# Attention beside a long convolution: the products of the last 128 convolution channels made later, and other paces for the convolution

## The chip, the cores and the metric

The kernel runs on one core of one Trainium2 chip. The metric is device time in microseconds (us); the median of seven runs of the kernel before is 862.89 us (860.53 to 865.09). One further execution was profiled. The engines are called PE (TensorE), ACT (ScalarE), DVE (VectorE), POOL (GpSimd) and SP (SyncE, which here only issues transfers).

## The reference

Two independent results stand side by side in the output, 512 columns each. The first is attention over 2048 positions with 32 heads of 16:

```python
qkv = (x @ wqkv).reshape(B, S, 3, H, Dh)           # S = 2048, H = 32, Dh = 16
p = softmax(einsum("bhqd,bhkd->bhqk", q, k) * Dh ** -0.5)
a = einsum("bhqk,bhkd->bhqd", p, v)  @ wo           # heads joined first
```

The second is a gated long convolution over 512 channels. The keys pass a causal filter of four taps, are multiplied by the values, and the product `kv` is convolved causally, channel by channel, with a filter as long as the sequence (in the reference by FFT):

```python
k_shift = sum(k_pad[:, t:t + S, :] * shift_k[:, 3 - t] for t in range(4))
kv = k_shift * v
y = causal_conv(kv, ssm_k) + kv * ssm_D             # 512 filters of 2048 taps
b = q * y
out = concatenate([a, b], axis=-1)
```

## The kernel before

**Attention.** Scores are cut into 2048 blocks of 128 keys by 512 queries (4 query blocks, 8 groups of 4 heads, 16 key tiles, 4 heads). A step T takes three blocks, or two: before step `N_EARLY` = 184 every odd step has two, later three steps in every 21 (the slots, which begin at step 190) and the last few. There are 741 steps. In a step `emit_qk` (line 539) makes the scores on PE, ACT makes the exponentials of the step in one instruction (line 550), and two steps later PE multiplies by the values (line 632). From step 56 on one of three blocks may go to DVE instead, which makes the exponential in five instructions (lines 586, 593 three times, 598); `dve_block` decides by how much work the planner has already given to DVE. When the sums of a group of heads are complete, DVE transposes them (line 696), divides by the row sum and, after two groups, transposes back into OTN (line 718). PE then multiplies by the output weights (line 749).

**Convolution.** The filters are reversed on DVE (`kz_turn`, line 426), with `ssm_D` added to one tap, and written to a scratch in DRAM (`kz_store`). From there SP loads, for each channel, 128 shifted copies of the filter, a row of WR of 512 KB. Four channels make a quad; three quads fit into WR, and `load_wr` issues the four loads of the next quad when a place comes free. `conv_lags` (line 804) makes the convolution of a quad as 16 lags, each of four small matmuls, one for each channel in its own quarter of PE. After eight quads `conv_turn` (line 830) transposes the result, and DVE multiplies it by q.

**The products kv.** The 512 channels are four blocks c of 128. A unit `("kv", c, i)` makes a quarter of a block: 16 matmuls (line 355) of the transposed keys in KTR with diagonal tap matrices DG, issued in two halves of eight, and one multiplication by the values on DVE (line 393). The buffers are shared with other things. KTR[0], for blocks 0 and 1, lies in QN; KTR[1], for blocks 2 and 3, lies in the second half of the query buffer QT. The values lie in WR, VS2 and OUTA. DG lies in rows 4 to 7 of OTN, one row for each block. Therefore the first write of the second half of QT (`evac_unit`, kind "q", qb = 1) and the transpose back for p = 4 (`turn_back`) wait for the last kv product (`h_kvm`). A quad of channels can only be convolved when all four kv units of its block are done.

**The order.** The program is written out in order by a planner in the kernel itself. Each engine has a planned clock; `us=(...)` in a call is what the planner counts for an instruction. `dma` counts a transfer as `kb/DMA_KB` us after the one before, or 3.6 us plus that after its issue. Units (v, k, q, kv, op, turn) are put in where there is room. `unit_step` takes the head of the list `early` before step 184 and issues half of it when `fits` says that it ends before the scores of the next step must start, with `SPARE` = 0.1 us to spare; a unit that is due is issued without room ("forced"). After step 184 units may only go into the slots, and `next_unit` takes the one with the earliest due time; in the steps 1 and 3 of a slot it is forced from 42 steps before its due time. `emit_bg` gives the convolution what is left: at most `LAGS` lags a step, as many as `room` allows (the end of the running exponential, less 0.47 us and `MARGIN`), and as many as the pace has credited. The credit grows by `PACE` times the lags left over the time left (1.14 us a step until 16 steps before the end), at most `RATE` = 3.4 lags/us. A quad is taken up only if its loads have landed by the planner's count. `KZ_LATE` is the time that the filter reversals wait after the filter has landed, by the same count.

All transfers of WR, and the transposing loads of keys and x, are issued by SP in program order; POOL issues the loads of q and of the output weights and most of the output. At the end `op_out_end` copies four tiles of the output, two on ACT (line 767) and two on DVE (line 769), and issues one transfer for each.

## Time and profile before

| | |
|---|---|
| median of 7 runs | 862.89 us (860.53 to 865.09) |
| the profiled execution | 869.32 us; its span 867.6 us, mean PE clock 0.977 |
| ACT busy | 837.7 us, 97% |
| DVE busy | 783.3 us, 90% |
| PE busy | 745.3 us, 86% |
| exponentials on ACT (line 550) | 741, of which 354 of three blocks (1569 ns) and 386 of two (1158 ns) |
| blocks on DVE (line 598) | 213 |
| matmuls of the convolution (line 804) | 8192 |
| loads of WR from the scratch | 512 of 512 KB, 8.0 us to landing (median) |
| DMA | 289.36 MB, mean 334 GB/s |
| kv units: DVE products (line 393) | 16, from 80.4 to 184.6 us; block 3 from 169.9 to 184.6 |
| PE waits for WR before line 804 | 10.7 us in 18 pieces, and 21.0 us before its weight loads |

Step 184 lies at about 205 us: the load of the output weights, which is issued there, starts at 205.2. "Busy" is the time in which an engine executes; PE's ends are modelled, and its weight loads are counted apart, since they run beside the matmuls. A time "from A to B" counts from the start of the span. The granted clock is the share of full speed that PE was given.

### The profile page before, as it was taken

Reading aid. Unit: us, or ns where it says so; the run is one execution under the profiler, and the core shown is the slowest. Engines: PE = TensorE matmul, PEld = TensorE weight load, DVE = VectorE, ACT = ScalarE, POOL = GpSimd, SP = SyncE. Lnnn points to the kernel's source line nnn. Section 1 sums busy time; section 2 is a strip of 40 time slices with the busy share of each in tenths; the row PEclk is TensorE's granted clock in tenths of the full one; section 3 lists DMA queues with packets and bytes.
Section 4 is the critical chain, followed back from the end, with each engine's and each line's share of the span. In section 5 each row is a group of like instructions: output and inputs, shape, how many; then the busy total and the mean of one; then the engine's idle time right before and its main releaser. Section 6 shows DMA issues by size and latency. Waiting matters only on the chain.

```text
span 867.6 us, 29386 instructions
## 1 busy us (share of the span) xinstructions
PE 745.3 (86%) x13146; PEld 304.8 (35%) x13184; DVE 783.3 (90%) x1330; ACT 837.7 (97%) x746; POOL 17.3 (2%) x33
## 2 busy tenths in 40 slices
PE   8888899998888888888888898888888888888877
PEld 2223343443333333333333323333333333333332
DVE  2328999999999999998999979989999999999994
ACT  6999999999999999998999979989999999999997
POOL 2000000000000000000000010000000000000000
PEclk9999999999999999999999969989999999999999
DMA  9960069779999999999999989989999999999942
GB/s 271 261 227 1 8 209 340 271 242 344 407 408 407 385 402 389 409 396 409 351 395 376 345 333 391 385 309 385 408 408 393 383 402 407 407 392 408 407 197 73
DMA packets 104813, 289.36 MB, mean 334 GB/s; under 512 B 35184, under 2 KB 37232, under 8 KB 104304
## 3 DMA queue, kind: packets, MB, share of 16 engines
q1 hardware_dynamic: 99424, 279.35, 85.8%
q0 software_dynamic: 1808, 6.29, 2.1%
q8 instruction: 104, 1.70, 0.8%
q10 hardware_dynamic: 3456, 1.84, 0.8%
q14 instruction: 21, 0.17, 0.1%
HBM read 276.83 MB, written 6.42 MB: 326 GB/s over the span
## 4 chain that ended last, share of the span: by engine, by line
ACT 62%; DVE 15%; PE 10%; DMA 9%; issue 2%; SPq 1%; ACTq 0%
ACT PT L550 62%; DMA WR<-kz_scratch 8%; DVE EH L593 7%; PE PS L539 4%; DVE FX L586 3%; DVE PTD L598 3%; PE PS L632 2%; PE PS L804 2%; SPq L223 1%; DVE QT L380 1%; DMA xT<-in_A_x_dram 1%; PE PS L363 1%; PE PS L749 1%; DVE DT L696 1%; PE PS L830 0%
## 5 line engine op out<-in xcount | busy, mean ns | idle before, releaser
L550 ACT ACTIVATE PT<-PS 128x1536 bf16<-128x1536 f32 (+1 forms) x741 | 834.7, 1354 | 17.7 <-PE PS L539 17.3
L539 PE MATMUL PS<-QT,KTo 32*128 32x512 bf16 x2048 | 306.9, 390 | 88.4 <-ACT PT L550 71.9
L593 DVE SCALAR_TENSOR_TENSOR EH<-EH,FX 128x512 f32<-128x512 f32 x426 | 285.4, 688 | 0.0
L804 PE MATMUL PS<-WR,KV 128*5 128x128 bf16 (+15 forms) x8192 | 224.0, 222 | 13.8 <-DMA WR<-kz_scratch 10.7
L632 PE MATMUL PS<-PT,VAF 128*32 128x512 bf16 x1835 | 203.8, 396 | 3.8 <-DVE DT L696 2.9
L804 PEld LDWEIGHTS PS<-WR,KV 128*2 128x2 bf16 (+15 forms) x8192 | 150.2, 88 | 98.8 <-issue 44.1
L539 PEld LDWEIGHTS PS<-QT,KTo 32*128 32x128 bf16 x2048 | 73.1, 91 | 268.9 <-ACT PT L550 228.1
L586 DVE TENSOR_SCALAR FX<-PS 128x512 f32<-128x512 f32 x213 | 147.3, 692 | 10.6 <-PE PS L539 10.3
L598 DVE SCALAR_TENSOR_TENSOR PTD<-EH,FX 128x512 uint16<-128x512 f32 x213 | 145.6, 686 | 0.0
L593 DVE SCALAR_TENSOR_TENSOR EH<-FX 128x512 f32<-128x512 uint16 x213 | 145.2, 691 | 0.0
L632 PEld LDWEIGHTS PS<-PT,VAF 128*32 128x32 bf16 x1835 | 48.6, 93 | 120.9 <-issue 108.2
L1012 PE MATMUL PS<-IDN,ZW 128*32 128x512 bf16 (+3 forms) x229 | 72.7, 318 | 1.2 <-DVE QN L839 0.9
L632 PE MATMUL PS<-PTD,VAF 128*32 128x512 bf16 x213 | 61.4, 390 | 0.0
L405 DVE CAST VAF<-PS 128x512 bf16<-128x512 f32 x16 | 11.1, 692 | 30.2 <-PE PS L363 30.2
L696 DVE STREAM_TRANSPOSE DT<-PS 128x512 f32<-128x512 f32 x31 | 22.3, 718 | 13.3 <-PE PS L632 12.6
L1012 PEld LDWEIGHTS PS<-IDN,ZW 128*32 128x32 bf16 x229 | 22.1, 97 | 12.0 <-issue 10.7
L380 DVE TENSOR_SCALAR QT<-PS,MASK 128x512 bf16<-128x512 f32 x30 | 21.2, 750 | 3.0 <-PE PS L335 2.8
L819 DVE CAST YB<-PS 128x512 bf16<-128x512 f32 x32 | 22.0, 689 | 0.6 <-PE PS L804 0.4
L363 PE MATMUL PS<-WKV,xT 128*128 128x512 bf16 x59 | 17.7, 383 | 2.6 <-DVE VAF L405 1.5
L749 PE MATMUL PS<-WKV,OTN 128*128 128x512 bf16 x53 | 17.7, 397 | 2.1 <-issue 1.1
L344 PE MATMUL PS<-xT,WKV 128*128 128x512 bf16 (+1 forms) x57 | 16.7, 376 | 2.0 <-issue 1.0
L335 PE MATMUL PS<-xT,WQ 128*128 128x512 bf16 x46 | 15.2, 388 | 2.4 <-issue 1.9
(66 smaller groups left out, 199.7 us busy)
## 6 DMA issues: line engine op xcount, KB each, us to landing
WR<-kz_scratch SPq DMA_DIRECT2D x512, 512.0 KB, 8.0
kz_scratch<-WR SPq DMA_DIRECT2D x1, 2176.0 KB, 8.5
QN<-in_B_q_dram POOLq DMA_DIRECT2D x2, 1024.0 KB, 12.7
out_dram<-QN POOLq DMA_DIRECT2D x2, 1024.0 KB, 7.5
out_dram<-OUTA POOLq DMA_DIRECT2D x12, 128.0 KB, 5.4
QN<-in_B_ssm_k_dram SPq DMA_DIRECT2D x1, 1024.0 KB, 6.2
QT<-in_B_ssm_k_dram SPq DMA_DIRECT2D x1, 1024.0 KB, 8.2
WR<-in_B_v_dram SPq DMA_DIRECT2D x2, 512.0 KB, 7.4
```

The source lines that it names most:

```text
L363: return e.matmul(PS[:, bank, :], lhsT=xT[:, dc, kt * 128:(kt + 1) * 128], rhs=WV[:, dc, :], start=(dc == 0), stop=(dc == 3))
L380: lambda e, par=par: e.tensor_scalar(QT[:, qb % 2, 2 * o + par, :], PS[:, bank, :], MASK[:, par:par + 1], None, ALU.mult),
L539: ins = e.matmul(PS[:, bank, :], lhsT=KTo[32 * s:32 * s + 32, g // 2, kt * 128:(kt + 1) * 128], rhs=QT[32 * s:32 * s + 32, qb % 2, g, :], ...
L550: h_exp[T] = act.op(lambda e: e.activation(PT[:, T % R_PT, 0:n * QB], PS[:, banks[0]:banks[0] + n, :].rearrange("p b f -> p (b f)"), ACT.E ...
L586: h_f = urgent(lambda e: e.tensor_scalar(fx, PS[:, bank, :], FIX_ADD, FIX_HI, ALU.add, ALU.min), [h, h_last.get(i - R_FX)], slack=0.6)
L593: st["h"] = dve.op(lambda e: e.scalar_tensor_tensor(eh, src, (A3, A2, A1)[j], frac, ALU.add, ALU.mult), [st["h"], h_last.get(i - R_EH), h_ ...
L598: lambda e: e.scalar_tensor_tensor(out16, eh, A4, fx, ALU.mult, ALU.add),
L632: ins = e.matmul(dst, lhsT=w, rhs=rhs, start=(k == 0), stop=(k == KT - 1), tile_position=(0, 32 * s))
L696: h_t = urgent(lambda e: e.transpose(out=dt, in_=PS[:, pvb(n), :]), [h] + before, slack=0.1, us=(0.63, 0.751))
L749: ins = e.matmul(PS[:, bank, :], lhsT=OTN[:, (4 * qb + o) % R_O, t * 128:(t + 1) * 128], rhs=WO[:, o, :], start=(o == 0), stop=(o == 3))
L804: ins = e.matmul(PS[32 * c:32 * c + NB - n, BGB, 128 * (kk % 4):128 * (kk % 4) + 128], lhsT=KV[:, qd, n:NB, c], rhs=WR[:, r + c, 128 * (NB ...
L1012: pe.op(lambda e: e.matmul(PS[32 * s:32 * s + 32, pvb(n), 0:128 * k], lhsT=ZW[:, :], rhs=rhs, start=False, stop=False, tile_position=(0, 3 ...
```

## The change

The key weights WK and the value weights WV change places in the buffer WKV, which gets 16 more columns. The keys of the convolution now come in three loads: blocks 0 and 1 as before (1024 KB), block 2 alone in the query buffer, and block 3 alone in the place of the key weights, which are no longer needed once the last key product k(3,3) is made; that load waits for this product. The values of blocks 2 and 3 change places. The four kv units of block 3 leave the list `early` and become jobs for the slots with the due time `KV_DUE` = 300. `h_kvm` is split: the query buffer and the transpose p = 4 wait for block 2, the transpose p = 7 for block 3.

Numbers: at most 5 lags a step instead of 6; PACE 1.15 instead of 1.2; before step 184 the lags keep a margin of 0.2 us instead of 0.35 (`EARLY_MARGIN`); KZ_LATE 8 instead of 4. At the end the transfer of output tile 1 is issued by SP instead of ACT.

```diff
--- before.py
+++ after.py
@@ -35,8 +35,8 @@
 PVB = 6
 BGB = 7
 N_EARLY = 184
-LAGS = 6
-PACE = 1.2
+LAGS = 5
+PACE = 1.15
 KEYS0 = 256
 END = 16
 
@@ -63,10 +63,12 @@
 GAP = 7
 TAIL_GAP = 4
 AHEAD = 4
-KZ_LATE = 4.0
+KZ_LATE = 8.0
 KEEP = 4
 BACKLOG = 3.9
 MARGIN = 0.35
+EARLY_MARGIN = 0.2
+KV_DUE = 300
 SPARE = 0.1
 DMA_KB = 400.0
 WINDOW = 3.4
@@ -175,7 +177,7 @@
     WQ = sb("WQ", [128, 4, D])
     PAT = sb("PAT", [1, 2, 128])
     MASK = sb("MASK", [128, 2], FP32)
-    WKV = sb("WKV", [128, 2, 4, D])
+    WKV = sb("WKV", [128, 8 * D + LEFT])
     OTN = sb("OTN", [128, R_O, QB])
     DT = sb("DT", [128, QB], FP32)
     DTN = sb("DTN", [128, 2, QB])
@@ -190,15 +192,17 @@
     EH = sb("EH", [128, R_EH, QB], FP32)
     ZW = sb("ZW", [128, 32])
     JNK = sb("JNK", [128, 2], FP32)
-    WK = WKV[:, 0, :, :]
-    WV = WKV[:, 1, :, :]
+    WK = WKV[:, 4 * D:8 * D].rearrange("p (c f) -> p c f", c=4)
+    WV = WKV[:, 0:4 * D].rearrange("p (c f) -> p c f", c=4)
     WO = WV
     VST = [x.rearrange("p (t d) -> p t d", t=NB)
-           for x in (WR[:, 8, :], WR[:, 9, :], VS2[:, :], OUTA[:, :, :].rearrange("p r d -> p (r d)"))]
+           for x in (WR[:, 8, :], WR[:, 9, :], OUTA[:, :, :].rearrange("p r d -> p (r d)"), VS2[:, :])]
     KZS = WRF[:, 0:4 * LKZ].rearrange("p (c m) -> p c m", c=4)
     DSS = WRF[:, 4 * LKZ:4 * LKZ + 4].rearrange("p (c m) -> p c m", m=1)
     KTR = [QNF[:, 0:2 * LKR].rearrange("p (c s) -> p c s", c=2),
-           QTF[:, NG * QB:NG * QB + 2 * LKR].rearrange("p (c s) -> p c s", c=2)]
+           QTF[:, NG * QB:NG * QB + LKR].rearrange("p (c s) -> p c s", c=1),
+           WKV[:, 4 * D:4 * D + LKR].rearrange("p (c s) -> p c s", c=1)]
+    KT_OF = [(0, 0), (0, 1), (1, 0), (2, 0)]
     DG = OTN[:, 4:8, :].rearrange("p t d -> p (t d)").rearrange("p (c m d) -> p c m d", c=4, m=4)
     KZN = [QTF[:, NG * QB:NG * QB + 2 * S].rearrange("p (c s) -> p c s", c=2),
            QNF[:, 0:2 * S].rearrange("p (c s) -> p c s", c=2)]
@@ -256,7 +260,7 @@
 
     d_w = [DmaSem(sem(f"d_w{i}")) for i in range(5)]
     d_x = [DmaSem(sem(f"d_x{i}")) for i in range(4)]
-    d_kv = [DmaSem(sem(f"d_kv{i}")) for i in range(6)]
+    d_kv = [DmaSem(sem(f"d_kv{i}")) for i in range(7)]
     d_tap, d_kz, d_kzw, d_wo = [DmaSem(sem(n)) for n in ("d_tap", "d_kz", "d_kzw", "d_wo")]
     d_q = [DmaSem(sem(f"d_q{i}")) for i in range(2)]
     d_outB = [DmaSem(sem(f"d_outB{i}")) for i in range(2)]
@@ -288,10 +292,10 @@
     h_vn, h_kt, h_kt0 = [], {}, {}
     for c in range(4):
         src = bass.AP(tensor=v2.tensor, offset=v2[128 * (NB - 1), 128 * c].offset, ap=[[D, 128], [-128 * D, NB], [1, 128]])
-        h_vn.append(dma(sp, d_kv[2 + c], VST[c], src, kb=1024))
+        h_vn.append(dma(sp, d_kv[3 + c], VST[c], src, kb=1024))
 
     def load_kt(i, dep):
-        h_kt[i] = dma(sp, d_kv[i], KTR[i][:, :, LEFT:LEFT + S], k2[:, 256 * i:256 * i + 256], [dep], transpose=True, kb=1024)
+        h_kt[i] = dma(sp, d_kv[i], KTR[i][:, :, LEFT:LEFT + S], k2[:, (0, 256, 384)[i]:(256, 384, 512)[i]], [dep], transpose=True, kb=(1024, 512, 512)[i])
         h_kt0[i] = pool.op(lambda e: e.memset(KTR[i][:, :, 0:LEFT], 0.0), [dep])
 
 
@@ -320,7 +324,7 @@
         if u[0] == "k":
             return h_x[u[2]] + [h_wk[min(u[1], 1)]]
         if u[0] == "kv":
-            return [h_kt[u[1] // 2], h_dg[0]]
+            return [h_kt[KT_OF[u[1]][0]], h_dg[0]]
         return h_x[u[1] // 4] + [h_wv]
 
     def pe_unit(u, bank, dcs=(0, 1, 2, 3)):
@@ -345,14 +349,15 @@
                                 rhs=xT[:, dc, sc * 512 + c0:(sc + 1) * 512], start=(dc == 0), stop=(dc == 3))
         elif kind == "kv":
             _, c, i = u
-            deps += [h_kt[c // 2], h_kt0[c // 2], h_dg[0]]
+            kt_i, kt_c = KT_OF[c]
+            deps += [h_kt[kt_i], h_kt0[kt_i], h_dg[0]]
             mm_us, mm_run = 0.27, 0.21
 
             def mm(e, b):
                 ins = None
                 for m in range(4):
                     c0 = LEFT + 128 * (4 * i + 3 - b) - m
-                    ins = e.matmul(PS[:, bank, 128 * b:128 * b + 128], lhsT=KTR[c // 2][:, c % 2, c0:c0 + 128], rhs=DG[:, c, m, :],
+                    ins = e.matmul(PS[:, bank, 128 * b:128 * b + 128], lhsT=KTR[kt_i][:, kt_c, c0:c0 + 128], rhs=DG[:, c, m, :],
                                    start=(m == 0), stop=(m == 3))
                 return ins
         else:
@@ -385,6 +390,8 @@
             hh = urgent(lambda e: e.tensor_copy(KTo[:, o, sc * 512 + c0:(sc + 1) * 512], PS[:, bank, c0:512]), [h],
                         us=(0.335, 0.46) if c0 else V512)
             h_k[(o, sc)] = hh
+            if (o, sc) == (3, 3):
+                load_kt(2, h)
         elif kind == "kv":
             _, c, i = u
             dst = KV[:, 32 * c:32 * c + 32, NB - 4 - 4 * i:NB - 4 * i, :]
@@ -396,8 +403,10 @@
                 load_qn(0, [h])
                 wr_free.append((2, hh))
                 load_wr()
-            if sum(kv_n) == 16:
+            if c == 2 and kv_n[c] == 4:
                 h_kvm[0] = h
+            if c == 3 and kv_n[c] == 4:
+                h_kvm[1] = h
         else:
             _, kt = u
             dst = VAF[:, kt, 0:H * VW].rearrange("p (h e) -> p h e", e=VW)[:, :, 0:DH]
@@ -408,7 +417,7 @@
 
     h_kvc = [None] * 4
     kv_n = [0] * 4
-    h_kvm = [None]
+    h_kvm = [None, None]
     wr_free = []
     wr_next = [0]
     h_kzw = [None]
@@ -715,10 +724,12 @@
                 deps += [h_op[((p - R_O) // 4, t)] for t in range(4)]
             if p == 4:
                 deps.append(h_kvm[0])
+            if p == 7:
+                deps.append(h_kvm[1])
             h_otn[(p, i1)] = h_otn[p] = dve.op(lambda e: e.transpose(out=OTN[:, p % R_O, sl], in_=dtn[:, sl]), deps, us=us)
 
         def may_turn():
-            return 2 * p in h_mul and 2 * p + 1 in h_mul and (p < R_O or all(((p - R_O) // 4, t) in h_op for t in range(4)))
+            return 2 * p in h_mul and 2 * p + 1 in h_mul and (p != 7 or kv_n[3] == 4) and (p < R_O or all(((p - R_O) // 4, t) in h_op for t in range(4)))
         u_r, u_m, u_t = (0.155, 0.28), (0.334, 0.46), (0.6, 0.75)
         if last:
             recip(u_r)
@@ -768,7 +779,7 @@
         else:
             hh = dve.op(lambda e: e.tensor_copy(dst, PS[:, bank, :]), [h])
         r0 = qb * QB + t * 128
-        dma(act if t % 2 else sp, d_outE, out2[r0:r0 + 128, 0:D], dst, [hh])
+        dma(act if t == 3 else sp, d_outE, out2[r0:r0 + 128, 0:D], dst, [hh])
 
 
     h_wr, h_qn = {}, {}
@@ -853,14 +864,14 @@
     early += [(91, ("k", 2, 0)), (92, ("q", 0, 2)), (98, ("k", 2, 1)), (104, ("k", 2, 2)), (110, ("k", 2, 3))]
     early += [(130, ("kv", 1, i)) for i in range(4)]
     early += [(137, ("q", 0, 3)), (138, ("k", 3, 0)), (144, ("k", 3, 1)), (150, ("k", 3, 2)), (155, ("k", 3, 3))]
-    early += [(N_EARLY - 4, ("kv", c, i)) for c in (2, 3) for i in range(4)]
+    early += [(N_EARLY - 4, ("kv", c, i)) for c in (2,) for i in range(4)]
     later_q = [("q", qb, o) for qb in range(1, NQB) for o in range(4)]
     later_op = [(qb, t) for qb in range(NQB - 1) for t in range(4)]
-    state = {"qd": 0, "lag": 0, "turn": False, "q": 0, "op": 0, "started": False, "lags": 0.0,
+    state = {"qd": 0, "lag": 0, "turn": False, "q": 0, "op": 0, "kv": 0, "started": False, "lags": 0.0,
              "left": C // 4 * NB, "t": 0.0}
 
     def room(T):
-        end = at(h_exp[min(T, NT - 1)]) - 0.47 - MARGIN
+        end = at(h_exp[min(T, NT - 1)]) - 0.47 - (EARLY_MARGIN if T < N_EARLY else MARGIN)
         return end - max(pe.t, at(bank_free[BGB]))
 
     def group_step(qb, g):
@@ -884,6 +895,8 @@
             u = later_q[st["q"]]
             if u[1] < 2 or (u[1] - 2) * NG + 2 * u[2] + 1 in pv_done:
                 jobs.append((group_step(u[1], 2 * u[2]), u))
+        if st["kv"] < 4:
+            jobs.append((KV_DUE, ("kv", 3, st["kv"])))
         return min(jobs) if jobs else None
 
     def fits(T, start, us):
@@ -1036,7 +1049,7 @@
         emit_bg(T)
         warm_up(T)
         advance(pe.t)
-    assert state["qd"] == C // 4 and not state["turn"] and state["q"] == len(later_q) and state["op"] == len(later_op), state
+    assert state["qd"] == C // 4 and not state["turn"] and state["q"] == len(later_q) and state["op"] == len(later_op) and state["kv"] == 4, state
     assert not early_dve and not flow and not acts and not dves
```

## The prediction

> **What bounds the kernel now.** I read the page first (shares, chain, groups), then the busy time in stretches of 20 us, then the worst stretch in steps of 2 us, then the waits.
>
> ```profile
> PE 745.3 (86%) x13146; PEld 304.8 (35%) x13184; DVE 783.3 (90%) x1330; ACT 837.7 (97%) x746; POOL 17.3 (2%) x33
> ...
> ACT 62%; DVE 15%; PE 10%; DMA 9%; issue 2%; SPq 1%; ACTq 0%
> ...
> L550 ACT ACTIVATE PT<-PS 128x1536 bf16<-128x1536 f32 (+1 forms) x741 | 834.7, 1354 | 17.7 <-PE PS L539 17.3
> ```
>
> ACT, which computes the exponentials (line 550), works 97% of the span, and the chain that ended last lies 62% on it. Each of the 2048 score blocks costs either ACT or DVE: 213 blocks go to DVE (five instructions each), the rest to ACT. A three-block exponential takes 1569 ns and a two-block one 1158, so a block is worth 411 ns of ACT. Nothing in the change alters how many blocks there are, so time can only come from ACT's idle time or from that split.
>
> ```profile
> 160.00:180.00 20.00, 19.14 (x311) 9.06 (x309) 19.89 (x35) 20.00 (x21) 0.00 (x0) 1.00 0.91 305
> ...
> 220.00:240.00 20.00, 17.45 (x369) 7.52 (x369) 19.35 (x34) 19.79 (x19) 0.00 (x0) 1.00 1.03 407
> ...
> 500.00:520.00 20.00, 18.09 (x185) 5.70 (x186) 13.91 (x23) 14.97 (x13) 2.88 (x3) 0.60 0.89 332
> ```
>
> Columns: stretch, length, busy time of PE, its weight loads, DVE, ACT and POOL with counts, granted PE clock, DMA share, GB/s. ACT is full at 160 to 180 us (and in each such stretch from 100 to 220), in the stage with the early units. Between 205 and 840 us it is busy 619.31 of 635.00 us, so 15.69 us are lost there, almost all in a few stretches such as 400 to 420 (2.45), 500 to 520 (5.03) and 560 to 580 (2.98). DVE is full nearly everywhere, and the DMA engines move about 407 GB/s at a share of 1.0 from 210 to 820 us, but only 305 at 160 to 180.
>
> ```profile
> 500.00:502.00 2.00, 1.60 (x30) 0.57 (x31) 2.00 (x4) 2.00 (x2) 0.00 (x0) 1.00 1.02 404
> 502.00:504.00 2.00, 0.82 (x18) 0.30 (x16) 2.00 (x5) 2.00 (x3) 0.00 (x0) 0.99 1.02 418
> 504.00:506.00 2.00, 2.00 (x33) 0.91 (x32) 0.54 (x1) 1.44 (x2) 0.00 (x0) 0.50 1.03 418
> 506.00:508.00 2.00, 2.00 (x18) 0.85 (x18) 0.70 (x2) 0.34 (x2) 0.20 (x1) 0.50 1.03 403
> ```
>
> PE was busy 0.82 of 2 us, then the granted clock was 0.50, and it stayed so until 520. In the timeline the cause is a wait of 0.93 us at 503.91 for a filter load (WR from kz_scratch).
>
> ```profile
> ACT PT L550 <- PE PS L539: 17.3, 32, 1.7
> ...
> PE PS L804 <- DMA WR<-kz_scratch: 10.7, 18, 1.5
> ```
>
> When ACT waits, it waits for the scores (PE line 539); PE in its turn stood 18 times before line 804, the convolution, for a filter load.
>
> ```profile
> 160.00:180.00 20.00, 3.91 (x140) 2.53 (x140) 1.00 0.91 305
> ...
> 220.00:240.00 20.00, 6.86 (x256) 4.43 (x256) 1.00 1.03 407
> ```
>
> These are the convolution's matmuls alone (line 804). A lag is 4 matmuls: 35 lags in 20 us before step 184, 64 in 20 us afterwards. A quad of channels has 16 lags and loads four rows of 512 KB, 2.097 MB; at 407 GB/s that is 5.15 us, so the queue carries at most 3.11 lags/us. Until 205 us only 201 lags are done (804 matmuls); the other 1847 run at the limit of the queue, and any late load stops PE.
>
> **The sum's base.** The profiled execution took 869.32 us, 1.72 more than its span, and 6.43 more than the median of 862.89. If that difference is stalls, an ordinary run loses 15.69 - 6.43 = 9.3 us between 205 and 840. By their stretches, 11.04 of the 15.69 follow a filter wait (220 to 240, 260 to 280, 400 to 420, 500 to 540, 640 to 660, 740 to 780, 800 to 820), and 4.65 do not, chiefly 560 to 580, where PE stood 1.80 us on "issue". Scaled by 9.3/15.69: 6.5 and 2.8 us.
>
> **The early lags (EARLY_MARGIN, the four moved units, LAGS, PACE).** The last four kv units leave the stage before step 184. A half unit is 8 matmuls and holds PE about 0.55 us:
>
> ```profile
> 167.40 0.62 PE L355 MATMUL PS<-OTN,QT 128*128 128x128 bf16 x8
> 167.95 0.39 PE L539 MATMUL PS<-QT,KTo 32*128 32x512 bf16 x2
> ```
>
> Four units are 8 halves, 4.4 us; with at most five lags a step they make room for up to 40 lags. The margin that lags keep before step 184 falls from 0.35 to 0.20 us, worth 0.15/0.055 = 2.7 lags a step by the kernel's own cost. What caps it is the pace: 1.15 x 2048 lags over 1.14 x (741 - 16 - 85) = 730 us is 3.23 lags/us, so at most some 355 lags in the 110 us before step 184. I take 300 of the range 201 to 355. Then 1748 are left over 1.14 x 541 = 617 us: the planner asks 1.15 x 1748/617 = 3.26 lags/us, and the wish falls under the queue's 3.11 after (1.15 x 1748 - 3.11 x 617)/(0.15 x 3.11) = about 195 us, at 400 us of the trace. Before, with 1847 left and pace 1.2, the same sum gives 683 us, and the trace shows a full queue until 820. So the part after some 400 to 550 us should lose its filter waits, and the costly ones of the profile lie there. Of the 6.5 us I take two thirds, 4.3 (bounds: 2.6, if only the waits after 640 and some before go, and 6.5, all). Of the 2.8 that stand on other causes between 0 and all may go with a calmer queue, since no row says what "issue" was; I take 0.7, nearer to nothing. What is late next is the exponential itself.
>
> **The clock.** The row above is the price of a filter wait: 0.93 us of waiting cost ACT 5.58 us in 500 to 540, because the clock stayed at 0.50 for 16 us. The Trainium skill (TensorE: Matmul & The Clock Gate, Part 1) says that the clock is halved after an idle window of about 3.4 us; no such idle window stands here, so by the rule waits this short would cost their length alone, some 1 us in all, and the sum would be about 861. The trace contradicts that, and the measured 0.50 decides.
>
> **The moved units' new place.** The due time is 300 and forcing begins 42 steps earlier, so they run in the slots between steps 253 and 300. PE: 4.4 us, beside 75 us in which PE and its weight loads wait for ACT from 205 to 400 (19.0 + 56.2). DVE: four evacuations of 0.69 us leave a full DVE before step 184 and enter a full DVE after it; a DVE block is five instructions of about 0.60 us, so 0.8 block is won early and lost late. Net 0, bounds -0.33 and +0.33. The units wait for a load that landed a hundred us earlier. Transpose p = 7 into OTN now waits for them, due at about step 380: 80 steps of cover.
>
> **The split key load.** Before: two transposing loads of 1 MB, when little else is needed from the queue.
>
> ```profile
> 27.91 6.21 SPq L223 DMA_TRANSPOSE QN<-in_B_k_dram  x1
> ...
> 34.79 9.60 SPq L223 DMA_TRANSPOSE QT<-in_B_k_dram  x1
> ```
>
> They held SP 6.21 and 9.60 us and landed in 8.3 and 13.1. Now the second is half as long, and the third, 512 KB, is issued after k(3,3), whose last product starts at 147.2 us (line 344), on SP's queue between filter loads. SP waits for that product, and the filter loads behind it wait too. By half of the rows it holds SP 3.1 to 4.8 us and lands in 4.2 to 6.5, while the planner counts 1.28. Cover: three slots of filters at then about 2.7 lags/us, 5.9 us a quad, so one loaded quad ahead hides it. I take 0 (bounds 0 and the rival below). The Trainium skill (DMA: Bandwidth & Descriptors, latency table) states 261 GB/s for such a transpose, 2.0 us for this size, which would hide even better; the rows decide. POOL gets one more memset of 0.12 us ahead of nothing urgent.
>
> **KZ_LATE.** The filter reversals (four of 0.64 us on DVE) start 4 us later. In the chain two of them, 1.20 us at 20.77, stand in front of a key evacuation, and ACT loses 0.40 us in 20 to 40. Gain 0 to 0.4, I take 0.2. The filter write moves from 34 to 38 us; the first lag runs at 95, with the DMA share at 0.00 from 60 to 80, so nothing is late.
>
> **The last output.** The copies on ACT start at 863.68 and 864.72, with 0.44 us between them for a DMA issue that now goes to SP. SP then issues three instead of two (0.94 for two). Gain 0 to 0.44, I take 0.3.
>
> **Sum:** -4.3 - 0.7 - 0.2 - 0.3 = -5.5, so 862.89 - 5.5 = 857.4 us. The bounds together: -2.6 + 0.33 and -6.5 - 2.8 - 0.4 - 0.44 - 0.33, so 852.4 to 860.6.
>
> **Rivals.** (1) The early stage takes no more lags; PE shows 19.14 of 20 us busy there, which speaks for it. Then pace 1.15 alone asks 1.15 x 1847/617 = 3.44 lags/us and the queue stays full until 644 us by the formula instead of 683. Perhaps 0.5 us of stalls go, with 0.5 for start and tail: 861.9, within 860.6 to 863.5.
> (2) Slower: the transposing load stalls the filters. If less than one quad lies ready at 148 us, PE waits up to 4.8 us there and then runs at clock 0.50 as at 504 to 520 (5.58): about +10, 857.4 + 10 = 867.4. It decides once it costs more than the 5.5 won, a stall near 1 us with a long half clock. Against it: 305 GB/s at 160 to 180, a queue with room.
> (3) Slower: the early steps are overfilled. If each of about 99 steps starts its exponential 0.1 us late, +9.9: 867.3; from 0.06 us a step on it eats the gain. Against it: the units already run with 0.1 us to spare in this stage, and ACT is at 20.00 of 20.00.
>
> **How the numbers follow.** Forecast 0.55, rival 1 0.20, rival 2 0.12, rival 3 0.13. About 0.2% (1.7 us) is what a measurement can tell from no change: 861.2 to 864.6. The forecast is faster throughout; rival 1 gives 0.05 faster, 0.14 the same, 0.01 slower; rivals 2 and 3 give 0.01 the same and 0.24 slower. So 0.60, 0.15, 0.25. The forecast's own range is 852.4 to 860.6; with the rivals, 852.5 to 868.0, which leaves out their upper ends.
>
> **What would show it.** Right: more than 270 lags (1080 matmuls of line 804) before step 184, ACT still full from 100 to 205 us, GB/s under 400 after some 550 us, fewer than 10 PE waits for filters, fewer stretches with clock under 1.0, and still about 213 DVE blocks. Wrong: a PE wait or a low clock at 148 to 165 us (rival 2), ACT idle spread over 100 to 205 (rival 3), the queue full until 820 (rival 1), or a DVE count off by more than ten, 4.1 us, which I did not foresee.

## The result and the profile after

The kernel after takes 873.15 us (median; 867.72 to 876.79), the kernel before 863.41 (856.93 to 870.87) on the same chip: a ratio of 1.0114, with a 95% interval of 1.0088 to 1.0139. It is 9.7 us slower where 5.5 us faster was forecast, and 873.15 lies above the range.

The profiled execution of after took 873.37 us (span 871.5), just its median. The profiled one of before took 869.32, 6 us above its median, so the two profiles differ by 4 us where the medians differ by 10. First the lines of the page that answer to those of before; the exponential is now line 559, the scores 548, the convolution 815, the turn 841, the output product 760.

```profile
PE 745.1 (85%) x13119; PEld 303.8 (35%) x13162; DVE 786.4 (90%) x1335; ACT 838.8 (96%) x746; POOL 17.4 (2%) x34
...
ACT 59%; PE 16%; DVE 11%; DMA 10%; issue 2%; SPq 1%
...
L559 ACT ACTIVATE PT<-PS 128x1536 bf16<-128x1536 f32 (+1 forms) x741 | 835.8, 1332 | 20.0 <-PE PS L548 19.2
```

ACT's work is the same (835.8 us of exponentials, 834.7 before) and 214 blocks went to DVE instead of 213: the time went into ACT's waits. The share of ACT in the chain fell from 62% to 59%, that of PE rose from 10% to 16%. The busy time in stretches of 20 us (columns as in the prediction):

```profile
140.00:160.00 20.00, 17.73 (x202) 5.93 (x203) 16.30 (x28) 17.27 (x17) 0.10 (x1) 0.91 1.05 353
160.00:180.00 20.00, 19.24 (x353) 9.21 (x351) 19.71 (x34) 20.00 (x21) 0.00 (x0) 1.00 0.88 268
220.00:240.00 20.00, 16.98 (x364) 7.56 (x353) 18.06 (x32) 18.93 (x16) 0.00 (x0) 1.00 1.02 383
280.00:300.00 20.00, 16.45 (x309) 6.79 (x310) 17.93 (x31) 18.28 (x17) 0.56 (x1) 0.83 0.94 347
360.00:380.00 20.00, 17.14 (x226) 5.71 (x231) 16.29 (x29) 16.67 (x16) 0.54 (x1) 0.74 0.79 310
500.00:520.00 20.00, 16.16 (x277) 6.12 (x278) 18.02 (x32) 18.88 (x17) 1.16 (x1) 0.91 1.02 384
```

At 140 to 160 us, where ACT had been full, it now loses 2.73 us; at 280 to 300 1.72; at 360 to 380 3.33, with the clock at 0.74. The stretch 500 to 520, the worst of before, loses 1.12. The queue moves 383 GB/s at 220 to 240, less than the 407 of before. ACT's idle time by stage, in us, from the same view:

| stage, us | before | after | e3 | e5 | e8 | e9 | e12 |
|---|---|---|---|---|---|---|---|
| 40–100 | 0.80 | 0.36 | 0.82 | 0.20 | 2.01 | 1.05 | 0.37 |
| 100–205 | 0.00 | 2.75 | 0.00 | 0.00 | 1.84 | 2.70 | 1.61 |
| 205–300 | 0.64 | 3.87 | 1.98 | 0.88 | 1.76 | 3.15 | 1.79 |
| 300–400 | 0.16 | 5.72 | 2.63 | 0.44 | 5.42 | 0.81 | 2.64 |
| 400–600 | 11.21 | 5.25 | 5.25 | 1.86 | 5.50 | 0.82 | 0.75 |
| 600–840 | 3.67 | 0.84 | 2.87 | 4.77 | 3.41 | 2.11 | 1.91 |

(e3 to e12 are experiments below. Each column is one execution: that of e8 lies 3.2 us above its median, that of e9 2.7 below, the others within 1.1 of theirs except before.) The new loss of after lies before 400 us: 12.3 us from 100 to 400, against 0.8. The 11.21 us of before at 400 to 600 belong to the profiled execution, 6 us above the median: e5, whose order is that of before but for one load, loses 1.86 there. The prediction's base for an ordinary run of before was 9.3 us between 205 and 840; after has 15.7 there, 2.8 more from 100 to 205, and 1.1 of ACT's work: 10.3 in all, against 9.7 measured. So the loss is almost all ACT's waiting, and the base held.

The waits of after (engine, line, what is waited for; us, times, longest):

```profile
ACT PT L559 <- PE PS L548: 19.2, 38, 1.5
...
PE PS L815 <- DMA WR<-kz_scratch: 12.5, 19, 1.6
```

The convolution's matmuls alone, by stretches (PE, weight loads, clock, DMA share, GB/s):

```profile
0.00:205.00 205.00, 26.49 (x936) 16.81 (x936) 0.99 0.74 230
160.00:180.00 20.00, 5.55 (x196) 3.49 (x196) 1.00 0.88 268
220.00:240.00 20.00, 7.56 (x247) 4.50 (x236) 1.00 1.02 383
```

There are 19 waits for filters before line 815 (18 before), and 936 matmuls until 205 us, 234 lags, where before had 201. So 33 lags came forward, not the 99 that I took.

**The first new wait, at 150 us.** After in steps of 2 us:

```profile
146.00:148.00 2.00, 2.00 (x13) 0.42 (x11) 1.97 (x4) 2.00 (x4) 0.00 (x0) 1.00 1.05 412
148.00:150.00 2.00, 0.37 (x8) 0.13 (x7) 0.91 (x2) 0.96 (x2) 0.00 (x0) 1.00 1.00 397
150.00:152.00 2.00, 1.67 (x13) 0.31 (x10) 0.77 (x2) 1.45 (x1) 0.00 (x0) 0.62 1.02 404
152.00:154.00 2.00, 2.00 (x8) 0.34 (x7) 0.82 (x2) 1.02 (x1) 0.00 (x0) 0.53 1.03 412
```

The instruction in PE's timeline (start, length, in brackets the idle time before it and what ended it):

```profile
149.80 0.24 PE L815 MATMUL PS<-WR,KV 128*16 128x128 bf16 x4 [1.63 <-DMA WR<-kz_scratch]
```

PE stands 1.63 us before the first lags of the eighth quad, whose filters have not landed. The clock is then 0.62 and 0.53, and ACT has 3.43 of 6 us from 148 to 154. The queue is full meanwhile (last column, 397 to 412 GB/s).

**The second, at 369 us.** PE's timeline of after; an output product is issued behind a turn:

```profile
367.32 0.62 PE L841 MATMUL PS<-IDN,YB 128*128 128x128 bf16 x8
369.40 0.63 PE L760 MATMUL PS<-WKV,OTN 128*128 128x512 bf16 x1 [1.46 <-DVE DR L712]
369.97 0.61 PE L548 MATMUL PS<-QT,KTo 32*128 32x512 bf16 x2
```

The same place in steps of 2 us:

```profile
368.00:370.00 2.00, 0.60 (x3) 0.17 (x4) 2.00 (x6) 1.20 (x1) 0.00 (x0) 0.73 1.02 408
370.00:372.00 2.00, 2.00 (x9) 0.30 (x8) 0.58 (x1) 1.02 (x1) 0.00 (x0) 0.50 1.03 410
372.00:374.00 2.00, 2.00 (x12) 0.35 (x11) 1.88 (x4) 1.02 (x1) 0.54 (x1) 0.50 1.01 401
```

The product's first matmul writes into a bank that DVE empties with line 850 at 368.26 to 368.94 us (the profile names the reciprocal after it; in e8 it names line 850 for the same wait). Everything behind it on PE, the next scores too, stands for 1.46 us, and the clock then stays at 0.50 until 378. The wait is in the kernel's own order: by the planner's clocks PE waits 1.15 us there. The unit was due, and a unit that is due is issued even where it doesn't fit. It came to stand there since units come later in this order: the four moved ones run at 194, 199, 221 and 246 us, the first output product at 293 instead of 260, and the one that waits, the fourth, at 369 instead of 312. The moved products are not needed for that: e1 below has the same wait without them.

**The transposing load** does what was expected of it, as SP's timeline of after shows:

```profile
155.95 3.87 SPq L227 DMA_TRANSPOSE WKV<-in_B_k_dram  x1
```

It holds SP 3.87 us and lands in 6.0. While it runs, at 158 to 164 us, the queue moves 156 to 180 GB/s instead of 400, but no lag waits there and ACT is full.

### The profile page after: what moved, and what is told of

Same layout as the page of the kernel before. It is cut to its first block, busy times and chain, and to the rows that moved or that the text cites. A ratio compares the mean times of both kernels' runs of the same rounds, so it can differ in the third digit from the quotient of the medians.

```text
span 871.5 us, 29319 instructions
## 1 busy us (share of the span) xinstructions
PE 745.1 (85%) x13119; PEld 303.8 (35%) x13162; DVE 786.4 (90%) x1335; ACT 838.8 (96%) x746; POOL 17.4 (2%) x34
## 3 DMA queue, kind: packets, MB, share of 16 engines
q10 hardware_dynamic: 3312, 1.71, 0.7%
## 4 chain that ended last, share of the span: by engine, by line
ACT 59%; PE 16%; DVE 11%; DMA 10%; issue 2%; SPq 1%
ACT PT L559 59%; DMA WR<-kz_scratch 10%; PE PS L548 6%; DVE EH L602 4%; PE PS L641 3%; PE PS L815 3%; DVE FX L595 2%; DVE PTD L607 2%; SPq L227 1%; DVE QT L385 1%; PE PS L760 1%; PE PS L360 1%; PE PS L368 1%; PE PS L461 1%; PE PS L348 0%
## 5 line engine op out<-in xcount | busy, mean ns | idle before, releaser
L559 ACT ACTIVATE PT<-PS 128x1536 bf16<-128x1536 f32 (+1 forms) x741 | 835.8, 1332 | 20.0 <-PE PS L548 19.2
L815 PE MATMUL PS<-WR,KV 128*15 128x128 bf16 (+15 forms) x8192 | 235.3, 222 | 17.8 <-DMA WR<-kz_scratch 12.5
L815 PEld LDWEIGHTS PS<-WR,KV 128*14 128x14 bf16 (+15 forms) x8192 | 153.1, 88 | 107.7 <-issue 51.2
L1025 PE MATMUL PS<-IDN,ZW 128*32 128x512 bf16 (+3 forms) x206 | 67.5, 328 | 0.4 <-DVE QN L850 0.4
L1025 PEld LDWEIGHTS PS<-IDN,ZW 128*32 128x32 bf16 x206 | 19.9, 96 | 9.5 <-issue 8.4
L390 DVE CAST KTo<-PS 128x512 bf16<-128x512 f32 (+1 forms) x16 | 10.7, 672 | 8.6 <-PE PS L348 8.5
```

Source lines behind the costliest of these rows:

```text
L559: h_exp[T] = act.op(lambda e: e.activation(PT[:, T % R_PT, 0:n * QB], PS[:, banks[0]:banks[0] + n, :].rearrange("p b f -> p (b f)"), ACT.E ...
L815: ins = e.matmul(PS[32 * c:32 * c + NB - n, BGB, 128 * (kk % 4):128 * (kk % 4) + 128], lhsT=KV[:, qd, n:NB, c], rhs=WR[:, r + c, 128 * (NB ...
L1025: pe.op(lambda e: e.matmul(PS[32 * s:32 * s + 32, pvb(n), 0:128 * k], lhsT=ZW[:, :], rhs=rhs, start=False, stop=False, tile_position=(0, 3 ...
```

## The experiments

Every ratio is to the kernel before on the same chip, with its 95% interval. First the cap, the constants and the structure.

**e1: the margin alone, on before.**

```diff
-        end = at(h_exp[min(T, NT - 1)]) - 0.47 - MARGIN
+        end = at(h_exp[min(T, NT - 1)]) - 0.47 - (EARLY_MARGIN if T < N_EARLY else MARGIN)
```

> The kernel before with EARLY_MARGIN = 0.2 alone (before step 184 the lags keep 0.2 instead of 0.35 us). Theory A (the early lags bring the convolution to the heels of its filter loads while only two of the three places for quads are free, and PE then waits and loses its clock): ratio to before 1.006 to 1.012, with a PE wait for a filter or a low clock between 100 and 200 us. Theory B (the moved units and the third key load cost the time): 0.998 to 1.002. Theory C (any other order of the program costs about as much, because the order before happened to be a good one): 1.004 to 1.012, with the stalls at places that differ from those of the changed kernel.

864.79 us, 1.0032 (0.9996 to 1.0067). PE waits 1.71 us for the eighth quad at 150 us, as in after, so this wait belongs to the margin, not to the moved products. The second wait is there too. All kv units of e1 have run by 197 us, yet the first output product runs at 288, and the fourth stands behind a turn (PE's timeline of e1; its line 750 is the output product, 840 the multiplication that empties the bank):

```profile
360.29 0.62 PE L831 MATMUL PS<-IDN,YB 128*128 128x128 bf16 x8
362.62 0.60 PE L750 MATMUL PS<-WKV,OTN 128*128 128x512 bf16 x2 [1.22 <-DVE QN L840]
```

In this execution, the fastest of e1's ten (861.90 us), the clock stayed at 1.00 after both, and ACT lost 1.54 us at 140 to 160 and 0.57 at 360 to 380. With both waits the margin by itself costs at most 0.7%; the median lies below the 1.006 to 1.012 of theory A.

**e2: the cap taken back.**

```diff
-LAGS = 5
+LAGS = 6
```

> The changed kernel with LAGS = 6 again, all else as changed. Theory A: still 1.008 to 1.014 of before, since the early lags stay. Theory B: the same, 1.008 to 1.014. Theory C: 1.004 to 1.012. A fourth, D (the cap of five lags leaves the convolution no way to catch up, so that it follows its loads more closely for the rest of the time): 0.998 to 1.004, with fewer filter waits than the changed kernel.

873.20 us, 1.0135 (1.0065 to 1.0204; four executions): as slow as after. The cap is not the cause. Its profile has the wait at 150 us (2.64), none at 369, and the second kind of wait in another place, a turn that waits for DVE in front of the scores; the planner's clocks have 2.1 us of waiting there. PE's timeline of e2:

```profile
615.04 1.03 PE L841 MATMUL PS<-IDN,YB 128*128 128x128 bf16 x8 [2.14 <-DVE QT L385]
```

The same place in steps of 2 us:

```profile
614.00:616.00 2.00, 0.96 (x8) 0.77 (x9) 1.58 (x3) 0.00 (x0) 0.00 (x0) 0.66 1.04 408
616.00:618.00 2.00, 2.00 (x26) 0.64 (x29) 1.89 (x4) 1.35 (x2) 0.00 (x0) 0.50 1.00 401
```

ACT does nothing from 614 to 616, and loses 6.40 us between 600 and 700.

**e3: the structure with before's numbers** (and the due time 260).

```diff
-LAGS = 5
-PACE = 1.15
+LAGS = 6
+PACE = 1.2
-KZ_LATE = 8.0
+KZ_LATE = 4.0
-EARLY_MARGIN = 0.2
-KV_DUE = 300
+EARLY_MARGIN = 0.35
+KV_DUE = 260
```

> The structure alone: kv units of the last block moved behind step 184, the third key load, the other places of the buffers and the last output on SP, with LAGS = 6, PACE = 1.2, EARLY_MARGIN = 0.35 and KZ_LATE = 4 as before; the due time is 260 instead of 300. Theory A: 0.997 to 1.003. Theory B: 1.007 to 1.014. Theory C: 1.004 to 1.012. Theory D: 0.997 to 1.003.

866.43 us, 1.0055 (1.0032 to 1.0078), in the range of theory C alone. This run does not test the products behind step 184: with these numbers and the due time 260 all four units of block 3 run before it, at 178 to 193 us in the trace, and the first output product at 241. What costs here is another order. There is no wait at 150 us (the margin is 0.35). The longest waits are for filters, 1.85 us at 217 and 1.42 at 319; the clock is 0.50 after each, and ACT loses 1.98 us at 210 to 230 and 1.76 at 310 to 330. PE's timeline of e3:

```profile
217.18 0.64 PE L815 MATMUL PS<-WR,KV 128*16 128x128 bf16 x24 [1.85 <-DMA WR<-kz_scratch]
```

Turns wait for DVE as well, 0.89 us at 488 and 0.79 at 705.

**e4: the numbers with before's structure.**

```diff
-LAGS = 6
-PACE = 1.2
+LAGS = 5
+PACE = 1.15
-KZ_LATE = 4.0
+KZ_LATE = 8.0
+EARLY_MARGIN = 0.2
```

> The numbers alone: LAGS = 5, PACE = 1.15, EARLY_MARGIN = 0.2 and KZ_LATE = 8 in the kernel before, with its structure. Theory A: 1.008 to 1.014. Theory B: 0.998 to 1.003. Theory C: 1.004 to 1.012. Theory D: 1.006 to 1.014.

865.16 us, 1.0020 (0.9983 to 1.0057). PE waits 1.93 us at 149 us. The numbers alone cost little. The excesses of e3 and e4 add up to 0.75%, short of the 1.14% of after, though the upper ends of their intervals would reach it; and since e3 does not hold the products behind step 184, the sum says little about them. Five lags with the margin of 0.35 was not tried by itself: with these two the planner does not place all lags before the end.

**e5: the third load and the buffers' places alone**, with before's order and numbers (and the last transfers as before).

```diff
-    early += [(N_EARLY - 4, ("kv", c, i)) for c in (2,) for i in range(4)]
+    early += [(N_EARLY - 4, ("kv", c, i)) for c in (2, 3) for i in range(4)]
-    state = {... "kv": 0, ...
+    state = {... "kv": 4, ...
```

> The third key load and the new places of the buffers alone: all units in the same order as before, the same numbers as before, the last output on ACT. PE's order of work is that of the kernel before. Theory B1 (the transposing load between the filter loads delays them, and PE waits): ratio to before 1.004 to 1.008, with a PE wait or a low clock at 148 to 175 us. Theory B2 (the moved units cost the time, where they now stand in the slots): 0.998 to 1.002.

861.38 us, 0.9980 (0.9941 to 1.0018). The load costs nothing that can be measured; rival 2 is out. It is on SP earlier than in after (SP's timeline of e5):

```profile
147.34 3.33 SPq L227 DMA_TRANSPOSE WKV<-in_B_k_dram  x1
```

and ACT stays full beside it (busy time of e5 by stretches):

```profile
140.00:160.00 20.00, 19.26 (x311) 8.39 (x314) 20.00 (x36) 20.00 (x21) 0.11 (x1) 1.00 0.95 311
```

**e6: after, with the four units back in the early stage.**

```diff
-    early += [(N_EARLY - 4, ("kv", c, i)) for c in (2,) for i in range(4)]
+    early += [(N_EARLY - 4, ("kv", c, i)) for c in (2, 3) for i in range(4)]
```

> The changed kernel with the last four kv units back in the list before step 184. Its order of lags is that of the run with the numbers alone (1.002), the third key load remains. Theory B1: 1.007 to 1.014. Theory B2: 1.000 to 1.005, and the ACT idle time between 205 and 400 us falls from the 9.6 us of the changed kernel to about 2.

865.51 us, 1.0017 (0.9979 to 1.0056). Without the moved units the rest of the change costs about what e1 and e4 cost, 0.97% less than after, and the two intervals lie apart. So with these numbers and this due time the loss comes with the moved units. ACT's idle time from 205 to 400 us is 1.5 us, as theory B2 said. The wait at 152 us is there (1.86).

**e7: after, with another due time.**

```diff
-KV_DUE = 300
+KV_DUE = 330
```

> The changed kernel with the due time of the moved units at 330 instead of 300; they come somewhat later among the other units, and the order of the program after step 184 differs. Theory B1: 1.007 to 1.014, as the changed kernel. Theory B2: the same, 1.007 to 1.014. Theory C (the cost lies in the accidents of one order): another value, between 0.998 and 1.008.

866.39 us, 1.0024 (0.9983 to 1.0064). The products are still moved (three run after 205 us instead of two), there are still five lags a step, and the wait at 150 us is even 2.51 us long; yet 0.9% of the 1.14% is gone. The output product behind a turn waits 0.94 us in place of 1.46, in a place where the planner's clocks have no wait of over 0.5, and the clock stays at 1.00 there. (The profiled execution, 860.30 us, is the fastest of e7's ten.) So it isn't the move by itself that costs, but the order that comes of it, as theory C said. This led to the next runs, which mend the two waits without moving the products.

**e8: the size of the q load put right.** The planner counts the load of q, 1024 KB by the page's list of transfers, as 512 KB. POOL issues it at 136.1 us, and all loads after it are planned 1.28 us too early. That is a part of the error only: in after the last filter of the eighth quad landed 12.8 us after the first was issued (136.9 to 149.8), where the planner counts 9.0; the three quads before it took 10.2, 9.8 and 9.1, where it counts 8.7. And the edit starts the eighth quad 2.3 us later by the plan, more than the 1.28.

```diff
-                      q2[:, 256 * i:256 * i + 256].rearrange("(t p) d -> p t d", p=128), deps)
+                      q2[:, 256 * i:256 * i + 256].rearrange("(t p) d -> p t d", p=128), deps, kb=1024)
```

> The changed kernel, with the load of q into QN counted by the planner at its true 1024 KB instead of 512. Up to about 550 us the order is that of the changed kernel except that the eighth quad starts 2.4 us later by the plan, so PE should no longer stand before its filter at 150 us. Theory E1 (the early margin costs through this one wait, 1.5 to 4.8 us of ACT's idle time between 100 and 205 us in every run with the margin of 0.2, none in those with 0.35): ratio to before 1.006 to 1.010 instead of 1.011 to 1.0135, and ACT's idle time from 100 to 205 us under 1 us. Rival (the wait there is hidden by what follows): 1.010 to 1.014.

870.76 us, 1.0082 (1.0047 to 1.0117). The wait at 150 us is gone, and ACT is full there (e8 in steps of 2 us):

```profile
148.00:150.00 2.00, 1.86 (x13) 0.42 (x11) 2.00 (x4) 2.00 (x3) 0.00 (x0) 1.00 1.01 391
150.00:152.00 2.00, 2.00 (x17) 0.52 (x16) 1.97 (x4) 2.00 (x3) 0.00 (x0) 1.00 1.05 414
152.00:154.00 2.00, 2.00 (x18) 0.52 (x13) 1.73 (x4) 2.00 (x3) 0.00 (x0) 1.00 1.03 410
```

The second wait is still there (1.05 us at 369.86), and the time fell by 0.3% only, within intervals that overlap. ACT's idle time from 100 to 205 us is 1.84 us, not under 1: it lies at 100 to 110, where this execution had a low clock, and at 195 to 205.

**e9: no unit after step 184 that would wait over 0.6 us** for its bank or its inputs, due or not.

```diff
-                if T < due or forced and N_EARLY <= T < stop:
+                if T < due or forced and N_EARLY <= T < stop or T >= N_EARLY and free - pe.t > 0.6:
```

> The changed kernel, in which a unit that is due in a slot is not forced while its PSUM bank is still to be emptied by DVE for more than 0.6 us. In the changed order one output product at 355 us by the plan (369 in the trace) is put in front of PE's other work and waits 1.15 us by the plan for DVE (1.46 in the trace), after which the clock is 0.50 for 12 us; the rule moves it. Theory E2 (forced units standing behind DVE are what the moved units cost): ratio 1.004 to 1.008, no low clock at 366 to 380. Rival (the thin stretches of PE in general, or the five lags, not this wait): 1.010 to 1.014.

866.32 us, 1.0051 (1.0012 to 1.0091; after's interval begins at 1.0088). The second wait is gone, and ACT has 19.88 of 20 us at 360 to 380 (16.67 in after). The first is there, 1.98 us, and this time the clock did not fall (e9 in steps of 2 us):

```profile
148.00:150.00 2.00, 0.99 (x8) 0.21 (x4) 1.73 (x3) 1.78 (x2) 0.00 (x0) 1.00 1.03 404
150.00:152.00 2.00, 1.03 (x12) 0.31 (x13) 0.00 (x0) 0.42 (x1) 0.00 (x0) 1.00 1.03 408
152.00:154.00 2.00, 2.00 (x14) 0.52 (x13) 1.79 (x3) 2.00 (x3) 0.00 (x0) 1.00 1.03 410
```

**e12: both.** The edits of e8 and e9 together.

> The changed kernel with the true size of the q load and the rule for forced units, one filler a step as before. If the two waits add up (0.3% and 0.6% of the 1.1%): ratio 1.000 to 1.005, mean clock 0.987 to 0.991. If the fillers did all the work in the run with all three: 1.005 to 1.010.

860.52 us, 0.9976 (0.9945 to 1.0007). With both waits mended the change costs nothing any more, and may be worth up to 0.5%; I had expected 1.000 to 1.005. Both stretches are full (e12, in stretches of 20 us):

```profile
140.00:160.00 20.00, 19.38 (x253) 7.20 (x250) 19.54 (x34) 20.00 (x20) 0.10 (x1) 1.00 1.06 349
360.00:380.00 20.00, 16.98 (x350) 7.19 (x336) 19.57 (x35) 19.88 (x19) 0.54 (x1) 1.00 1.02 386
```

The two waits are 5.9 of the 12.3 us that ACT lost in after from 100 to 400 us. Both edits move other units too: ACT's idle time at 205 to 300 us, where neither wait lies, falls from 3.87 to 1.79. And e7 gained 0.9% by another order, with the first wait still there. So it is shown that the order of after cost the 1.1%, and that these two edits to the planner take it away; that the two waits are all of it isn't shown.

**e10, e11, e13, e14: more filler.** `warm_up` puts matmuls of zeros into gaps of PE. Three calls in place of one, on e12 (e10), on e5 with the two mends of e8 and e9 (e11), on e5 alone (e13) and on after alone (e14):

```diff
-        warm_up(T)
+        for _ in range(3):
+            warm_up(T)
```

> The changed kernel with both of these and up to three fillers a step instead of one (matmuls of zeros where PE would wait for ACT). Theories E1 and E2 together with E3 (PE's thin stretches before a wait let the clock fall): ratio 0.992 to 1.000, mean clock above 0.992. If only the stalls matter and not the fill: 1.000 to 1.004 and a clock near 0.988.

861.42 us, 0.9994 (0.9951 to 1.0036): nothing gained over e12, and a median clock of 0.990 where above 0.992 was expected.

> The kernel of the run with the third key load alone (order and numbers of the kernel before), with the rule for forced units and up to three fillers a step. Theory E3: ratio 0.991 to 0.997, mean clock above 0.994, since the kernel before loses about 6 us to a clock of 0.989. Rival (fillers delay the scores as much as they save): 0.998 to 1.004.

857.63 us, 0.9926 (0.9894 to 0.9958): 0.7% faster than the kernel before. It keeps the products early and the numbers of before. Its page:

```profile
PE 758.2 (89%) x13284; PEld 308.0 (36%) x13284; DVE 782.6 (91%) x1330; ACT 836.0 (98%) x746; POOL 17.4 (2%) x34
...
ACT 73%; PE 10%; DMA 10%; DVE 5%; SPq 1%; issue 1%; ACTq 0%
```

> The kernel of the third key load alone with up to three fillers a step, without the rule for forced units. The kernel before loses about 6 us to a clock of 0.989. If the fillers are what made the run with load, rule and fillers fast (0.9926): 0.991 to 0.996, clock above 0.993. If it was the rule: 0.996 to 1.001 and a clock of 0.990.

859.43 us, 0.9956 (0.9933 to 0.9978): 0.44 of the 0.74% of e11 comes without the two mends; whether these add to it on before's order is not settled, since the intervals overlap.

> The changed kernel with up to three fillers a step and nothing else; the order of its lags is the same up to 550 us. Its two waits, at 150 and at 369 us, stay; the fillers can only keep the clock up around thin stretches. Expected 1.003 to 1.008 with a clock of 0.985 to 0.990, if about half of the 11 us that the clock costs goes; 1.009 to 1.013 if the clock falls because of the waits alone.

868.00 us, 1.0069 (1.0036 to 1.0101): 0.45% below after, with intervals that overlap. Fillers may ease the waits' cost; they do not remove it.

**The two parts of the time.** Over the executions of the kernel before that ran beside the experiments, the time follows the mean granted clock: 857.1 us + 554 us x (1 - clock), with a residual of 1.5 us. If the other kernels are held against this line, what they take above it is time that the clock doesn't explain:

| kernel | waits in it | part of the clock, us | above the line, us |
|---|---|---|---|
| before | neither | about 6 | 0 |
| after | both | 10.9 | 4.7 |
| e8 | second | 11.6 | 2.2 |
| e9 | first | 8.7 | 1.4 |
| e12 | neither | 5.2 | -1.2 |
| e7 | first, and 0.94 us of the second | 7.7 | 1.0 |
| e2 | first, and one at 615 us | 10.9 | 5.3 |
| e1 | both | 6.0 | 3.1 |
| e4 | first | 6.1 | 2.1 |
| e6 | first | 5.5 | 3.1 |
| e3 | neither | 7.1 | 2.3 |
| e5 | neither | 5.0 | -0.4 |
| e14 | both, fillers | 7.3 | 4.8 |
| e10 | neither, fillers | 6.3 | -1.0 |
| e13 | neither, fillers | 2.0 | -0.5 |
| e11 | neither, fillers | 1.8 | -1.2 |

From after to e8, e9 and e12, mending the first wait takes 2.5 us off the last column, the second 3.3, both 5.9: they add (each value is good to some 0.2 to 0.9 us, a difference to about 1). The other orders scatter by as much: e3, with neither wait, lies 2.3 above the line, e7, with the first, 1.0. In after's order the clock's part falls by half only when both are gone; yet e1, with both, has no more of it than before, so the two waits alone don't set it. What else in the order of after lowers the clock stays open. The fillers of e14 work on the clock's part alone. That the line holds for other kernels than before is assumed, not shown.

## Why the prediction was wrong

**"The early lags" failed, and it was the main term (-5.0 with the calmer queue).** I took 300 lags before step 184 from a pace formula. The trace has 234 until 205 us; the planner's own bookkeeping has 245 by step 184, where before it had 198. By the same bookkeeping what holds the convolution in quads 2 to 7, up to 147 us, is not the room on PE but the filters: two of the three places of WR are free at first, the third holds values of blocks 0 and 1 until their products are made. With a smaller margin the lags only catch up with the loads: the planned slack of quads 2 to 7 fell from 3.3, 1.4, 7.5, 6.1, 11.5 and 7.6 us to between 1.4 and 2.3. At that distance the planner's error becomes a wait: the last filter of the eighth quad came 3.8 us later after its first issue than planned, of which the size of the q load is 1.28; the rest isn't explained. The kernel's text says that a quad is taken up only if its loads have landed by the planner's count; I did not ask how well that count is met. The queue stayed full to 820 us (407 GB/s at 800 to 820) where I expected under 400 from 550 on, so rival 1 described the later part: no calmer queue, 19 filter waits where I named fewer than ten. In e12, without the two waits, the gain is 2.1 us (0.24% of 862.86; the interval reaches from 4.7 to -0.6), not 5.5.

**"The moved units' new place", net 0 with bounds of 0.33 us, failed.** I counted the time of the four units on PE and DVE and the loads that they wait for, and put them between steps 253 and 300. Two of them ran before step 184 after all, at 194 and 199 us, and two in the first slots, at 221 and 246. I had no term for the order that comes of the move. The slots are a queue ordered by due times: what does not fit early comes due before it fits, and then waits at the head of PE; e9 forbids such waits and gets back 0.6%. With the units back in the early stage the loss is 0.97% smaller (e6), with another due time 0.9% (e7): the price of this move lies between nothing and some 8 us, by its order alone. The wait of the output product is not the moved products' own, for the smaller margin alone brings it about (e1, 1.22 us). There ACT lost 0.57 us at 360 to 380, in after, where the clock fell, 3.33; why it fell in one and not in the other stays open.

**"The clock" was right in kind.** The wait of 1.63 us cost ACT 2.57 us from 148 to 154, that of 1.46 cost 3.33 from 360 to 380. The Trainium skill (TensorE: Matmul & The Clock Gate, Part 1) speaks of an idle window of about 3.4 us before the clock is halved; it was halved here after waits of half that length, so the trace decides again. But I counted on waits going away and did not price new ones by the same row: a single wait at the price of 5.58 cancels the whole gain of 5.5.

**Rivals.** Rival 2 (the transposing load) was wrong: e5. My price of it, 3.1 to 4.8 us on SP and 4.2 to 6.5 to landing, held (3.87 and 6.0). But the sign that I named for it, "a PE wait or a low clock at 148 to 165 us", appeared from another cause, before the load was issued (155.95): a sign that two causes share decides nothing. Rival 3 (overfilled early steps, 867.3) had the right sign and a wrong reason: ACT is not a little late in each step from 100 to 205 us, it loses 2.57 of its 2.75 us there from 148 to 154 and is full from 155 to 200.

**Small terms.** ACT's work and the 214 DVE blocks came out as said. KZ_LATE's 0.2 us didn't show: ACT's idle time in the first 40 us is 7.66 before and 8.09 after, and between 7.36 and 8.44 in all runs with either value. The last transfer's 0.3 can't be told apart in the runs. Stretches with a low clock were to become fewer; after has seven, the profile of before six.

**The range** was built from the terms that I had. Its upper end, 868.0, came from rivals with one stall (rival 2) or one spread delay (rival 3); several stalls in one kernel were in no case.

## What to carry to other kernels

In a program whose order is written out by a planner, a moved unit or a smaller margin is paid for in the order behind it: print the order of everything behind it, and look for instructions that are issued before their buffer is free. Before a margin is cut, ask how far the planned times are from the measured ones; here the slack of one quad fell from 7.6 to 2.1 us, and an error of 3.8 us, a third of it from a transfer counted at half its size, became a wait. And before a wait is put down to one edit, look for it in the runs without that edit. Both mends here are one line each and turn a loss of 1.1% into none; fillers and the mends on before's order give 0.7%.

## What the runs showed of the hardware

- One hundredth of mean granted clock goes with 5.5 us in this kernel (554 us x 0.01), and more matmuls of zeros can raise it: the median clock was 0.992 for e5 with 229 such matmuls and 0.9975 for e13 with 342, 0.980 for after with 206 and 0.986 for e14 with 310. From e12 (210) to e10 (308) it did not rise (0.9905 and 0.9895).
- The clock fell after waits of 0.93 us (before), 1.46 and 1.63 us (after), not always: the 1.98 us of e9 and the 1.71 of e1 left it at 1.00. And it fell without a long wait, where PE is merely thinly busy. In after, PE has 1.14 and 1.21 of 2 us (its longest wait there is 0.95 us, for ACT), and the clock is halved:

```profile
284.00:286.00 2.00, 1.14 (x14) 0.27 (x14) 2.00 (x4) 2.00 (x3) 0.00 (x0) 1.00 1.02 408
286.00:288.00 2.00, 1.21 (x26) 0.48 (x26) 2.00 (x6) 2.00 (x3) 0.00 (x0) 0.75 1.03 412
288.00:290.00 2.00, 2.00 (x33) 0.84 (x30) 1.93 (x4) 2.00 (x2) 0.00 (x0) 0.50 1.02 408
```

- Some of PE's waits have no cause in the profile. In after:

```profile
312.47 0.22 PE L815 MATMUL PS<-WR,KV 128*13 128x128 bf16 x1 [2.26 <-issue]
```

In e8 there is one of 2.19 us at 678.5. Such waits of over 1 us occur in after and in e8, e9 and e12 between 199 and 315 us, and none of over 1 us in e3, e5 or e7. The 1.80 us of before at 573 is of the kind. In after, e9 and e12 one stands before the same matmul (line 815, 128*13, a single one; 2.26, 1.59 and 1.98 us), so it isn't chance alone. What they are stays open; they are part of what e12 still loses.
- While the transposing load of 512 KB runs in after, the queue moves 156 to 180 GB/s for some 6 us (158 to 164 us).
